# One activation-table set for Ln and Exp, chosen by the kernel: retention attention followed by a channel mix

## The chip, the core and the metric

The kernel runs on one core of one Trainium2 chip. The metric is device microseconds of one execution, as the median of the runs of a kernel; lower is better. Engines are called by the names that the profile uses: PE (TensorE), DVE (VectorE), ACT (ScalarE), POOL (GpSimd) and SP (the queue that issues the stores). PEld is the weight load of a matmul, which overlaps PE.

## The reference: what is computed

```python
def _attn_ref(q, k, v, g_norm):            # (8, 8, 576, 64) each, g_norm (64,)
    kv = np.einsum('bhsd,bhse->bhde', k, v)
    out = np.einsum('bhsd,bhde->bhse', q, kv)
    rms = np.sqrt(np.mean(out * out, axis=-1, keepdims=True) + 1e-06)
    return (out / rms * g_norm).astype(np.float32)

def _moe_ref(x, mu_k, mu_r, w_k, w_v, w_r):  # x (8, 576, 512), F = 1024
    x_prev = x shifted by one position, zero first
    xk = mu_k * x + (1.0 - mu_k) * x_prev
    xr = mu_r * x + (1.0 - mu_r) * x_prev
    k = np.maximum(xk @ w_k, 0.0)
    v = k * k @ w_v
    r = 1.0 / (1.0 + np.exp(-(xr @ w_r)))
    return (r * v).astype(np.float32)
```

The attention's output, heads side by side, is the x of the channel mix. Inputs and output are float32; the kernel works in bf16 with float32 sums.

## The kernel before, in words

The work comes in two kinds of pieces. `attention(b)` makes batch b ready: its k, v and q come by POOL's DMAs (L277); PE multiplies k by v into "kv" (L374) and transposes q (L402); PE multiplies q by kv (L421, "u"); copies take the results from PSUM to the tiles kvb, qT and uT (helper `copy`, L195 to L199, on ACT or on DVE); DVE squares u (L435); PE sums the squares over each head (L447, "ss"); ACT computes ln(ss/64 + 1e-6) (L450, `ln_act`) and exp(-0.5 ln), the reciprocal root (L453, `exp_act`), into the tile rs; DVE multiplies (L468, xT), takes differences (L479) and blends them with mu (L493, L496) into the rings xk and xr. All this is in pairs of heads: four pairs ("hp") in a batch, so four ln and four exp.

`mix(g)` takes 512 of the 4608 rows: k (L548, 32 matmuls), relu on ACT (L552), square on DVE (L555), r (L574, 16 matmuls), sigmoid on ACT (L578, `r_sig`), v (L601, 32 matmuls), the product with the sigmoid on DVE (L605, "out"), and the stores by SP (L531). There are nine groups g and eight batches b.

PSUM has two rings of two buffers each: "mm" for the mix, "at" for the attention. A kv, q or ss matmul has to wait until the "at" buffer of two pieces earlier has been read, which for ss is by ln; a k or v matmul waits in the same way for relu, sigmoid or out. The tile rs has one buffer.

The order of the instructions on each engine is written by `Planner` (L31 to L127). It takes every piece with its engine, an assumed duration and a due time, and picks the earliest. It knows two tables, "ln" and "sig" (pieces carry `table="ln"` or `table="sig"`), and adds `TABLE = 1.3` to a piece that changes between them; ln and exp have the same one. The order is then fixed, engine by engine. In the middle of the kernel one batch and one group are done in each round: sigmoid, then ln, ln, exp, exp twice (two pairs of heads each time), then relu and copies.

ACT computes functions from a table that has to be loaded (ACT_TABLE_LOAD). The kernel before asks for one load itself, at the start (L250, the set `natural_log_exp_and_others`, which holds both Ln and Exp); the other loads are put in by the compiler ahead of an ACTIVATE whose function is not in the set it last loaded. Those stand in the profile under the line of that ACTIVATE.

Of the kernel before, what the change touches and what calls it, by code (L numbers as in the profile page):

```python
# [30 lines left out]
class Planner:  # L31
# [10 lines left out]
    def add(self, on, fn, deps=(), bufs=(), due=0.0, rel=0.0, land=0.0, mode=None, table=None, name=""):  # L42
        p = Piece(on, fn, deps, bufs, due, rel, land, mode, table, name)
        self.left.append(p)
        return p
# [85 lines left out]
def kernel(  # L131
# [13 lines left out]
    nc = tc.nc  # L145
# [38 lines left out]
    add = plan.add  # L184

    def get(buf, dtype=None):
        if buf.t is None:
            n, shape, dt = BUFS[buf.tag]
            if dtype is not None:
                dt, shape = dtype, shape[:-1] + (shape[-1] * 2,)  # L190
            pool = psum if buf.tag in ("mm", "at") else sb
            buf.t = pool.tile(list(shape), dt, tag=buf.tag, name=buf.tag, bufs=n)
        return buf.t

    def copy(eng, dst, src):  # L195
        if eng == "ACT":
            nc.scalar.copy(out=dst, in_=src)  # L197
        else:
            nc.vector.tensor_copy(out=dst, in_=src)  # L199

    def act_us(n, sbuf=False, ap=False):
        return 0.1 + n / 1200 + (0.03 if sbuf else 0.0) + (0.09 if ap else 0.0)

# [28 lines left out]
    def first_load(n, eng):  # L232
        def fn(_):
            e = nc.sync if eng == "SP" else nc.scalar
            e.dma_start(out=first[n], in_=part(n, 0, 0, 2))
        return add({eng: 0.36}, fn, due=-2000, land=0.72, name="first" + n)

    def setup(_):
# [8 lines left out]
    f_k = first_load("k", "SP")  # L247
    f_v = first_load("v", "ACT")
    f_q = first_load("q", "SP")
    add({"ACT": 1.3}, lambda _: nc.scalar.preload_act_table_set("natural_log_exp_and_others"), due=-1999,  # L250
        table=None, name="table")
    p_set = add({"DVE": 1.4}, setup, due=-1999, name="setup")

    def small_loads(_):
# [8 lines left out]
    def cast(n, due):  # L263
        def fn(eng):
            copy(eng, get(kvq[(n, 0)])[:, 0:2, :], first[n])
        p = add({"DVE": dve_us(768, 2), "ACT": act_us(768, True)}, fn,
                deps=[{"k": f_k, "v": f_v, "q": f_q}[n], p_set], bufs=[kvq[(n, 0)]], due=due, name="cast" + n)
        for h in range(2):
            loaded[(n, 0, h)] = p
# [34 lines left out]
    def scale_w(dst, dep, due, name, on):  # L304
# [5 lines left out]
        return add(on, fn, deps=[dep, p_cols], due=due, name=name)  # L310

    both = {"DVE": dve_us(2048, 4), "ACT": act_us(2048, True, True)}
    p_wr = scale_w(w_r_sb, load_w(w_r_sb, moe_w_r, -700, 2.6, "w_r"), -50, "g.w_r", {"DVE": both["DVE"]})
    p_wk = []
# [25 lines left out]
    def attention(b):  # L340
# [9 lines left out]
        def when(stage, hp, pos=0):  # L350
            off, spread = STAGES[stage]
            if b == 0:
                return {"due": -200 + 6 * hp + off, "rel": 0.0}
            t = base + off + spread * hp
            return {"due": t, "rel": t - 4.0 if b > 2 else 0.0}
# [9 lines left out]
        for hp0, n in groups[1 if fine else 2 if b == 1 else 4]:  # L365
            ps = warm_ps if fine else Buf("at")
            hps = range(hp0, hp0 + n)
            o, bank = (HD * hp0, 1) if fine else (0, 0)

            def kv_mm(_, hps=hps, hp0=hp0, ps=ps, o=o, bank=bank):  # L370
                for hp in hps:
                    for j in range(NJ):
                        for e in range(2):
                            nc.tensor.matmul(  # L374
                                get(ps)[64 * e:64 * e + 64, bank, o + HD * (hp - hp0):o + HD * (hp - hp0) + HD],
                                kin.t[:, 2 * hp + e, HD * j:HD * j + HD], vin.t[:, 2 * hp + e, HD * j:HD * j + HD],
                                start=(j == 0), stop=(j == NJ - 1))

            def kv_cp(eng, e, hp0=hp0, n=n, ps=ps, o=o, bank=bank):
                rows_ = slice(64 * e, 64 * e + 64)  # L380
                copy(eng, kv[rows_, hp0:hp0 + n, 64 * e:64 * e + 64],
                     ps.t[rows_, bank, o:o + HD * n].rearrange("q (i d) -> q i d", d=HD))

            mm = add({"PE": 0.25 * n + 0.02}, kv_mm, bufs=[ps, kin, vin], mode="kv", name=f"kv{b}.{hp0}",
                     deps=[loaded[(m, b, h)] for m in ("k", "v") for h in (2 * hp0, 2 * (hp0 + n) - 1)],
                     **when("kv", hp0))
            cps = [add({"DVE": dve_us(64 * n), "ACT": act_us(64 * n)}, lambda eng, e=e, f=kv_cp: f(eng, e),
                       deps=[mm, p_set] + users, bufs=[ps], name=f"kvc{b}.{hp0}", **when("kvc", hp0))
                   for e in range(2)]
            for hp in hps:  # L390
                kvc[hp] = cps

        for hp0, n in groups[1 if fine else 2]:
# [11 lines left out]
            def q_cp(eng, hp0=hp0, n=n, ps=ps):  # L405
# [6 lines left out]
                    name=f"qc{b}.{hp0}", **when("qc", hp0))  # L412
# [3 lines left out]
        for hp in range(NHP):  # L416
# [7 lines left out]
            def u_cp(eng, hp=hp, ps=ps):  # L424
# [6 lines left out]
                         name=f"uc{b}.{hp}", **when("uc", hp))  # L431

        for hp0, n in groups[1 if b <= 1 else 2]:
            def u_sq(_, hs=slice(hp0, hp0 + n)):
# [3 lines left out]
                    name=f"sq{b}.{hp0}", **when("sq", hp0))  # L438
# [3 lines left out]
        for hp in range(NHP):  # L442
            ps, ln = Buf("at"), Buf("ln")

            def ss_mm(_, hp=hp, ps=ps):
                for i in range(2):
                    nc.tensor.matmul(get(ps)[:, i, 0:HS], ones, sq.t[:, hp, HS * i:HS * i + HS], start=True, stop=True)  # L447

            def ln_act(_, ps=ps, ln=ln):
                nc.scalar.activation(out=get(ln), in_=ps.t[:, :, 0:HS], func=AF.Ln, bias=eps, scale=1.0 / HD)  # L450

            def exp_act(_, hp=hp, ln=ln):
                nc.scalar.activation(out=get(rs)[:, hp].rearrange("q (i c) -> q i c", i=2), in_=ln.t, func=AF.Exp,  # L453
                                     scale=-0.5)

            m = add({"PE": 0.25}, ss_mm, deps=[sqc[hp], p_set], bufs=[ps, sq], mode="full", name=f"ss{b}.{hp}",
                    **when("ss", hp))
            a = add({"ACT": act_us(S, False, True)}, ln_act, deps=[m], bufs=[ps, ln], table="ln", name=f"ln{b}.{hp}",
                    **when("ln", hp))
            exps[hp] = add({"ACT": act_us(S, True)}, exp_act, deps=[a], bufs=[ln, rs], table="ln",  # L460
                           name=f"exp{b}.{hp}", **when("exp", hp))
# [72 lines left out]
    def mix(g):  # L534
# [23 lines left out]
        for f2 in range(NFC // 2):  # L558
            ps, rt, u = Buf("mm"), Buf("relu"), k0 + 2 * f2
            ms = []  # L560
            for x in range(2):
                ms.append(add({"PE": 0.865}, lambda _, fc=2 * f2 + x, ps=ps: k_mm(_, fc, ps),
                              deps=ms or need["k"] + [p_wk[f2 // 2]], bufs=[ps, sqk], due=u + x, mode="full",
                              name=f"k{g}.{2 * f2 + x}"))
            a = add({"ACT": act_us(1024)}, lambda _, ps=ps, rt=rt: k_relu(_, ps, rt), deps=ms[1:], bufs=[ps, rt],
                    due=u + 2, name=f"relu{g}.{f2}")
# [8 lines left out]
                                 start=(cc == 0), stop=(cc == NHP - 1))  # L575

        def r_sig(_, ps, sg):
            nc.scalar.activation(out=get(sg), in_=ps.t, func=AF.Sigmoid)  # L578

        sigs = []  # L580
        for c2 in range(2):
            ps, sg, u = Buf("mm"), Buf("sig"), r0 + 2 * c2
            ms = []
            if g == 0 and c2 == 0:
                for cc in range(NHP):
                    ms.append(add({"PE": 0.43}, lambda _, cc=cc, ps=ps: [r_mm(_, x, ps, [cc]) for x in range(2)],
                                  deps=ms[-1:] + [need["r"][cc], p_wr], bufs=[ps], due=u + 0.2 * cc, mode="full",
                                  name=f"r{g}.p{cc}"))
                ms = ms[-2:]
            else:  # L590
                for x in range(2):
                    ms.append(add({"PE": 0.865}, lambda _, ci=2 * c2 + x, ps=ps: r_mm(_, ci, ps, range(NHP)),
                                  deps=ms or need["r"] + [p_wr], bufs=[ps, sg], due=u + x, mode="full",
                                  name=f"r{g}.{2 * c2 + x}"))
            sigs.append((sg, add({"ACT": act_us(1024)}, lambda _, ps=ps, sg=sg: r_sig(_, ps, sg), deps=ms[1:],
                                 bufs=[ps, sg], due=u + 2, table="sig", name=f"sig{g}.{c2}")))
# [10 lines left out]
        for c2 in range(2):  # L607
# [3 lines left out]
            for x in range(2):  # L611
                for part_ in range(2):
# [3 lines left out]
                                  due=u + 2 * x + part_, mode="full", name=f"v{g}.{2 * c2 + x}.{part_}"))  # L616
# [45 lines left out]
```

## Time and profile before

| | |
|---|---|
| median of 3 runs | 249.96 us (249.74 to 249.97) |
| the profiled execution: its time | 250.53 us |
| its span | 248.8 us |
| busy: PE | 212.2 us (85%) |
| busy: ACT | 168.1 us (68%) |
| busy: DVE | 152.8 us (61%) |
| busy: POOL | 28.2 us (11%) |

The span is what the profiler sees from the first to the last instruction; the time has 1.73 us more around it. In a row of the timeline the first number is the start in us, the second the length of all instructions of the row together, then come the engine, the line, the operation, the tiles (out<-in), how many instructions were merged, and in brackets the idle time of the engine before it with what ended that idle time.

### The profile page before, as it was taken

The page shows a single profiled execution, that of the slowest core. Times are in us where ns is not written, and L with a number is a line of the kernel's source. Part 1 is how long each engine was busy: PE and PEld are TensorE (multiplying, and loading weights), DVE is VectorE, ACT ScalarE, POOL GpSimd, SP SyncE. Part 2 cuts the span into 40 slices and gives each one's busy share as a digit, 9 for nine tenths or more (in the row PEclk, how much of TensorE's full clock was granted, in tenths as well). Part 3 has the DMA queues.
Part 4 walks back from the last instruction along what each step waited for, and adds up shares of the span by engine and source line. Part 5 has one row for each costly group of instructions (what it writes and reads, how often), then busy time and mean ns, then how long its engine had stood idle before and what let it go on. Part 6 is the DMA issues. An engine that isn't in the chain of part 4 may idle for free.

```text
span 248.8 us, 4251 instructions
## 1 busy us (share of the span) xinstructions
PE 212.2 (85%) x1730; PEld 111.1 (45%) x1730; DVE 152.8 (61%) x287; ACT 168.1 (68%) x198; POOL 28.2 (11%) x43
## 2 busy tenths in 40 slices
PE   6784799598895859999699969996998999999981
PEld 6552345255442424455345656553453444444430
DVE  3279757479548668956991789369927943314221
ACT  2376349979799996899469957994899732513600
POOL 8932303023100001102010000000000000000000
PEclk9999999979998998999889999999999999999997
DMA  7999999999990229903990320033003205006023
GB/s 173 197 203 206 203 203 205 209 189 192 227 177 1 55 77 163 161 3 85 190 181 0 87 84 3 0 87 86 0 3 93 76 0 163 8 10 162 0 84 84
DMA packets 27431, 26.93 MB, mean 108 GB/s; under 512 B 1804, under 2 KB 22804, under 8 KB 27412
## 3 DMA queue, kind: packets, MB, share of 16 engines
q0 software_dynamic: 21008, 16.34, 43.6%
q1 hardware_dynamic: 6196, 10.04, 14.5%
q10 hardware_dynamic: 208, 0.29, 0.4%
q8 instruction: 13, 0.21, 0.3%
q14 instruction: 6, 0.05, 0.1%
HBM read 33.56 MB, written 9.44 MB: 173 GB/s over the span
## 4 chain that ended last, share of the span: by engine, by line
PE 45%; ACT 28%; DVE 15%; issue 5%; DMA 4%; SPq 1%; DVEq 0%; ACTq 0%
PE mm L548 18%; PE mm L601 11%; PE mm L574 8%; ACT L450 7%; ACT ln L450 7%; ACT rs L453 4%; ACT L453 3%; PE at L402 3%; ACT sig L578 2%; PE at L421 2%; DVE md L493 2%; DVE out L605 2%; DMA rows<-in_g_norm_dram 2%; DVE xr L496 2%; DVE qT L199 2%
## 5 line engine op out<-in xcount | busy, mean ns | idle before, releaser
L548 PE MATMUL mm<-xk,w_k 128*128 128x512 bf16 (+1 forms) x320 | 70.7, 367 | 3.6 <-DVE w_k L309 1.4
L601 PE MATMUL mm<-w_v,sqk 128*128 128x512 bf16 x288 | 68.9, 392 | 4.7 <-ACT sig L578 3.1
L552 ACT ACTIVATE relu<-mm 128x1024 bf16<-128x1024 f32 x36 | 36.7, 1022 | 38.3 <-PE mm L548 37.7
L605 DVE TENSOR_TENSOR out<-mm,sig 128x1024 f32<-128x1024 f32 (+1 forms) x20 | 22.3, 1116 | 40.8 <-PE mm L601 16.6
L601 PEld LDWEIGHTS <-sqk 128*128 128x128 bf16 x288 | 28.8, 100 | 38.3 <-issue 9.6
L548 PEld LDWEIGHTS <-w_k 128*128 128x128 bf16 x320 | 30.3, 99 | 32.8 <-issue 4.9
L574 PE MATMUL mm<-w_r,xr 128*128 128x512 bf16 x144 | 33.4, 379 | 3.7 <-DVE xr L496 2.8
L555 DVE TENSOR_TENSOR sqk<-relu 128x1024 bf16<-128x1024 bf16 x36 | 24.7, 687 | 14.7 <-ACT relu L552 14.5
L197 ACT CAST uT<-at 128x576 bf16<-128x576 f32 x24 | 15.0, 638 | 12.7 <-PE at L421 12.4
L468 DVE TENSOR_TENSOR xT<-uT,rs 128x1152 bf16<-128x1152 bf16 (+1 forms) x18 | 12.4, 690 | 17.9 <-ACT rs L453 17.9
L450 ACT ACTIVATE ln<-at,eps 128x576 f32<-128x576 f32 x32 | 22.4, 738 | 1.1 <-PE at L447 0.8
L578 ACT ACTIVATE sig<-mm 128x1024 bf16<-128x1024 f32 x18 | 18.2, 1024 | 7.0 <-PE mm L574 6.9
L574 PEld LDWEIGHTS <-xr 128*128 128x128 bf16 x144 | 13.8, 98 | 19.8 <-DVE xr L496 3.9
L493 DVE TENSOR_SCALAR md<-d,cols 128x576 bf16<-128x576 bf16 x64 | 21.2, 368 | 0.3
L453 ACT ACTIVATE rs<-ln 128x576 bf16<-128x576 f32 x32 | 20.5, 677 | 0.3
L453 ACT ACT_TABLE_LOAD x16 | 20.5, 1283 | 0.3
L450 ACT ACT_TABLE_LOAD x16 | 20.5, 1283 | 0.3
L421 PE MATMUL at<-qT,kvb 128*128 128x288 bf16 x64 | 13.8, 300 | 8.0 <-DVE qT L199 6.4
L277 POOL DMA_DIRECT2D k<-in_k_dram x11 | 8.1, 737 | 66.3 <-PE at L374 63.3
L435 DVE TENSOR_TENSOR sq<-uT 128x1152 bf16<-128x1152 bf16 (+1 forms) x20 | 12.6, 633 | 3.0 <-ACT uT L197 2.7
L199 DVE COPY qT<-at 128x1152 bf16<-128x1152 bf16 (+1 forms) x16 | 11.2, 700 | 3.7 <-PE at L402 3.6
L402 PE MATMUL at<-ident,q 96*64 96x96 bf16 x384 | 13.2, 223 | 0.0
(47 smaller groups left out, 161.5 us busy)
## 6 DMA issues: line engine op xcount, KB each, us to landing
out_dram<-out SPq DMA_DIRECT2D x24, 192.0 KB, 2.4
k<-in_k_dram POOLq DMA_DIRECT2D x6, 576.0 KB, 7.8
v<-in_v_dram POOLq DMA_DIRECT2D x6, 576.0 KB, 10.9
q<-in_q_dram POOLq DMA_DIRECT2D x6, 576.0 KB, 9.1
out_dram<-out SPq DMA_DIRECT2D x24, 128.0 KB, 2.4
out_dram<-out SPq DMA_DIRECT2D x24, 64.0 KB, 2.0
w_k<-in_moe_w_k_dram POOLq DMA_DIRECT2D x2, 512.0 KB, 10.5
w_v<-in_moe_w_v_dram POOLq DMA_DIRECT2D x1, 1024.0 KB, 15.9
```

Of the source, the lines that this page charges most:

```text
L402: nc.tensor.transpose(t[64 * e:64 * e + 64, hp - hp0, NP * j:NP * j + NP], qin.t[:, 2 * hp + e, HD * j:HD * j + HD], ident[:NP, :NP])
L421: nc.tensor.matmul(get(ps)[:, i, 0:HS], kv[:, hp, :], qT.t[:, hp, HS * i:HS * i + HS], start=True, stop=True)
L450: nc.scalar.activation(out=get(ln), in_=ps.t[:, :, 0:HS], func=AF.Ln, bias=eps, scale=1.0 / HD)
L453: nc.scalar.activation(out=get(rs)[:, hp].rearrange("q (i c) -> q i c", i=2), in_=ln.t, func=AF.Exp, scale=-0.5)
L493: nc.vector.tensor_scalar(out=get(md)[:, hp], in0=d.t[:, hp], scalar1=cols[:, m0 + hp:m0 + hp + 1], scalar2=None, op0=ALU.mult)
L548: nc.tensor.matmul(get(ps)[:, fc % 2, a0:a1], w_k_sb[:, cc, 128 * fc:128 * fc + 128], xk[:, cc, x0:x0 + a1 - a0], start=(cc == 0), stop=(c ...
L552: nc.scalar.activation(out=get(rt), in_=ps.t, func=AF.Relu)
L555: nc.vector.tensor_mul(out=get(sqk)[:, 2 * f2:2 * f2 + 2, :], in0=rt.t, in1=rt.t)
L574: nc.tensor.matmul(get(ps)[:, ci % 2, :], xr[:, cc, n0:n0 + 128], w_r_sb[:, cc, :], start=(cc == 0), stop=(cc == NHP - 1))
L578: nc.scalar.activation(out=get(sg), in_=ps.t, func=AF.Sigmoid)
L601: nc.tensor.matmul(get(ps)[:, ci % 2, :], sqk.t[:, fc, 128 * ci:128 * ci + 128], w_v_sb[:, fc, :], start=(fc == 0), stop=(fc == NFC - 1))
L605: nc.vector.tensor_mul(out=get(ot)[:, xs, :], in0=ps.t[:, xs, :], in1=sg.t[:, xs, :])
```

## The change

A helper `table(name)` remembers the set that the kernel asked for last, and asks for another one only where the name differs. It is called ahead of every Ln and Exp with `natural_log_exp_and_others`, ahead of every Sigmoid with `sigmoid_and_others`, and for the load at the start.

```diff
+    loaded_table = [None]
+
+    def table(name):
+        if loaded_table[0] != name:
+            loaded_table[0] = name
+            nc.scalar.preload_act_table_set(name)
...
-    add({"ACT": 1.3}, lambda _: nc.scalar.preload_act_table_set("natural_log_exp_and_others"), due=-1999,
-        table=None, name="table")
+    add({"ACT": 1.3}, lambda _: table("natural_log_exp_and_others"), due=-1999, name="table")
...
             def ln_act(_, ps=ps, ln=ln):
+                table("natural_log_exp_and_others")
                 nc.scalar.activation(out=get(ln), in_=ps.t[:, :, 0:HS], func=AF.Ln, bias=eps, scale=1.0 / HD)
 
             def exp_act(_, hp=hp, ln=ln):
+                table("natural_log_exp_and_others")
                 nc.scalar.activation(out=get(rs)[:, hp].rearrange("q (i c) -> q i c", i=2), in_=ln.t, func=AF.Exp,
                                      scale=-0.5)
...
         def r_sig(_, ps, sg):
+            table("sigmoid_and_others")
             nc.scalar.activation(out=get(sg), in_=ps.t, func=AF.Sigmoid)
```

On ACT, in a round in the middle of the kernel, this stands in the queue before (sig is the sigmoid of a group, ln and rs the logarithm and the exponential of a batch, x2 two pairs of heads):

```order
L578 ACT_TABLE_LOAD
L578 ACTIVATE sig<-mm 128x1024 x2
L450 ACT_TABLE_LOAD
L450 ACTIVATE ln<-at,eps 128x576 x2
L453 ACT_TABLE_LOAD
L453 ACTIVATE rs<-ln 128x576 x2
L450 ACT_TABLE_LOAD
L450 ACTIVATE ln<-at,eps 128x576 x2
L453 ACT_TABLE_LOAD
L453 ACTIVATE rs<-ln 128x576 x2
L197 CAST kvb_74<-at 64x4x64
```

And this is the same place with the change (its lines are numbered a little higher, and all loads have the line of the helper):

```order
L206 ACT_TABLE_LOAD
L587 ACTIVATE sig<-mm 128x1024 x2
L206 ACT_TABLE_LOAD
L457 ACTIVATE ln<-at,eps 128x576 x2
L461 ACTIVATE rs<-ln 128x576 x2
L457 ACTIVATE ln<-at,eps 128x576 x2
L461 ACTIVATE rs<-ln 128x576 x2
L197 CAST kvb_74<-at 64x4x64
```

Three of the five loads of the round are gone, and nothing has changed places. Over the whole queue of ACT, 14 loads stand where 40 stood: 1 at the start, 7 ahead of sigmoids, 6 ahead of a Ln. PE, DVE, POOL and SP have the same instructions in the same order as before.

## Prediction

> **What bounds the kernel now.** I read the page first: the busy times, the engine shares of the chain that ended last, and the groups of table loads.
>
> ```profile
> PE 212.2 (85%) x1730; PEld 111.1 (45%) x1730; DVE 152.8 (61%) x287; ACT 168.1 (68%) x198; POOL 28.2 (11%) x43
> ...
> PE 45%; ACT 28%; DVE 15%; issue 5%; DMA 4%; SPq 1%; DVEq 0%; ACTq 0%
> ...
> L453 ACT ACT_TABLE_LOAD x16 | 20.5, 1283 | 0.3
> L450 ACT ACT_TABLE_LOAD x16 | 20.5, 1283 | 0.3
> ```
>
> The groups by line of ACT give the other loads.
>
> ```profile
> L578 ACT ACT_TABLE_LOAD x7 | 9.0, 1283 | 0.1
> ...
> L250 ACT ACT_TABLE_LOAD x1 | 1.3, 1283 | 1.2 <-PEq L646 1.2
> ```
>
> 40 loads of 1.283 us are 51.3 of ACT's 168.1 us. ACT is not the busiest engine, but it is 28% of the chain. So the question is where PE, the busiest, stands still because of ACT. PE's waits:
>
> ```profile
> PE at L421 <- DVE qT L199: 6.4, 3, 2.2
> PE at L374 <- ACT ln L450: 5.7, 2, 2.9
> PE mm L601 <- ACT sig L578: 3.1, 1, 3.1
> ```
>
> The first is ACT at second hand, as the rounds below show: that DVE copy is late because DVE waited for rs.
>
> **The change.** It removes 26 loads (14 stay), 26 x 1.283 = 33.4 us of ACT. It moves nothing, adds no wait, and no DMA is touched. What is gained is not 33.4 but what PE no longer waits; so I went along the timeline and asked at each wait of PE what is late next. First, Ln and Exp from the joint set cost nothing extra. In batch 0, both run from it already; the chain of waits has
>
> ```profile
> 13.68 0.75 ACT ln L450
> 14.46 0.69 ACT rs L453
> ```
>
> against 0.74 and 0.68 for the later ones (45.50 below, and half of 1.37 for a pair), and exp starts 0.03 us after the ln that it reads. So a removed load is worth its whole slot on ACT.
>
> *Group 0 and batch 1, to 55 us.* The timeline:
>
> ```profile
> 44.21 1.28 ACT L450 ACT_TABLE_LOAD   x1
> 45.50 0.74 ACT L450 ACTIVATE ln<-at,eps 128x576 f32<-128x576 f32 x1
> 46.26 1.28 ACT L453 ACT_TABLE_LOAD   x1
> 48.26 1.28 ACT L450 ACT_TABLE_LOAD   x1
> 49.55 1.37 ACT L450 ACTIVATE ln<-at,eps 128x576 f32<-128x576 f32 x2
> 50.34 0.95 PE L374 MATMUL at<-v,k 96*64 96x64 bf16 x48 [2.78 <-ACT ln L450]
> 52.03 3.23 PE L601 MATMUL mm<-w_v,sqk 128*128 128x512 bf16 x8
> ...
> 83.20 1.89 PE L601 MATMUL mm<-w_v,sqk 128*128 128x512 bf16 x8
> ```
>
> The kv matmul at 50.34 waits for the first ln of the pair. The ln at 45.50 comes 1.28 earlier with the load at 44.21 gone, and I add 0.3 because the copy in front of it also moves up; then two more loads go: 1.28 + 0.3 + 2 x 1.28 = 4.1. What is late next is PE itself (eight v matmuls and an ss that also sat behind ln), which I put 0.4 later: **+3.7**. Behind this wait the eight matmuls at 52.03 took 3.23 us, where the same eight at 83.20 took 1.89: they ran at half speed after PE stood still. With the wait gone I count 3.23 - 1.89 = **+1.3**. Then DVE becomes late: its xT, d, xr and out rows run on without a gap, and the squares that feed the next ss come, by my count, 1.2 after PE wants them: **-1.2**. Sum 3.8.
>
> *Group 1, to 83 us.*
>
> ```profile
> 60.24 1.28 ACT L450 ACT_TABLE_LOAD   x1
> ...
> 62.29 1.28 ACT L453 ACT_TABLE_LOAD   x1
> ...
> 65.23 1.02 PE L548 MATMUL mm<-xk,w_k 128*128 128x512 bf16 x4 [1.02 <-ACT relu L552]
> ...
> 71.15 1.28 ACT L450 ACT_TABLE_LOAD   x1
> ...
> 73.21 1.28 ACT L453 ACT_TABLE_LOAD   x1
> ...
> 77.57 5.30 PE L601 MATMUL mm<-w_v,sqk 128*128 128x512 bf16 x16 [3.06 <-ACT sig L578]
> ```
>
> The two loads ahead of 65.23 (2.6 us) hide PE's wait of 1.02 for relu entirely: **+1.0**. The v matmuls at 77.57 wait for the sigmoid; two loads go in front of it, 2.57, of which I take 2.3 (a Ln waits for its ss instead): **+2.3**, and PE keeps a wait of 0.7. The sixteen at 77.57 took 5.30 at half speed against 3.6 (twice 1.89, less their overlap): **+1.7**. Sum 8.8.
>
> *Batch 3, to 107 us.*
>
> ```profile
> 81.13 1.28 ACT L453 ACT_TABLE_LOAD   x1
> ...
> 85.78 0.41 PE L447 MATMUL at<-sq,ones 128*128 128x288 bf16 x2 [0.69 <-ACT ln L450]
> ...
> 88.95 1.28 ACT L450 ACT_TABLE_LOAD   x1
> ...
> 91.03 0.95 PE L374 MATMUL at<-v,k 96*64 96x64 bf16 x48 [2.88 <-ACT ln L450]
> ...
> 91.92 3.26 PE L548 MATMUL mm<-xk,w_k 128*128 128x512 bf16 x8
> ```
>
> Four loads go from 81.13 to 88.95, 5.1 us of ACT, more than the two waits of PE (0.69 + 2.88); about 0.3 stays, because the ss ahead has to come first: **+3.3**. The eight at 91.92 are at half speed again, 3.26 - 1.89 = **+1.4**. From there to 107 DVE works without a gap, and the second copy of qT comes 0.7 after PE wants it: **-0.7**. Sum 12.8.
>
> *The rounds of batches 4 to 6, then batch 7.* Of the round of batch 5 the timeline has:
>
> ```profile
> 135.95 1.28 ACT L453 ACT_TABLE_LOAD   x1
> 138.51 1.28 ACT L450 ACT_TABLE_LOAD   x1
> 138.53 0.76 DVE L468 TENSOR_TENSOR xT<-uT,rs 128x1152 bf16<-128x1152 bf16 x1 [1.06 <-ACT rs L453]
> 143.78 0.76 DVE L468 TENSOR_TENSOR xT<-uT,rs 128x1152 bf16<-128x1152 bf16 x1 [0.85 <-ACT rs L453]
> 148.23 0.41 PE L421 MATMUL at<-qT,kvb 128*128 128x288 bf16 x2 [2.07 <-DVE qT L199]
> ```
>
> Three loads go from the round, so the second rs comes 3.85 earlier, but DVE has its own work: it only loses its two waits, 1.06 + 0.85 = 1.91. Everything from the second xT to the qT copy is DVE without a gap, so u comes 1.9 earlier and PE's 2.07 becomes about 0.2. I take **+1.9** for the round of batch 4 and **+1.85** each for the next two. In the round of batch 4 the wait of u was 2.21 and slow matmuls followed, in the others not:
>
> ```profile
> 122.66 0.41 PE L421 MATMUL at<-qT,kvb 128*128 128x288 bf16 x2 [2.21 <-DVE qT L199]
> ...
> 124.10 1.89 PE L548 MATMUL mm<-xk,w_k 128*128 128x512 bf16 x4
> ```
>
> Four of those are 1.03 at 65.23 above; with the transposes beside them **+1.1**. Sum 12.8 + 1.9 + 1.1 + 3.7 = 19.5. In batch 7 the wait that matters is
>
> ```profile
> 191.47 4.69 PE L548 MATMUL mm<-xk,w_k 128*128 128x512 bf16 x21 [1.20 <-DVE out L605]
> ```
>
> an "out" that sits behind the xT that waits for rs: **+1.1**. From 191.47 on PE has only mix matmuls and nothing changes. Total **20.6 us**: span 248.8 - 20.6 = 228.2, time 250.53 - 20.6 = **229.9 us** by the profiled execution's own time, which is 0.57 above the median of the runs shown; against that median I would say 229.4 and keep 229.9.
>
> The Trainium skill ("ScalarE: Activation LUTs", What ACT_TABLE_LOAD costs) gives a switch 1283 ns for the load and about 1380 ns more for a drain, 2.66 us in all; by that the 26 loads would free an estimated 69 us of ACT and not 33.4. The trace agrees with the 1283 and shows no drain: the load at 46.26 starts 0.02 after its ln ends, and the pair of ln at 49.55 starts 0.01 after the load.
>
> Half-speed matmuls are 1.3 + 1.7 + 1.4 + 1.1 = 5.5 of the 20.6. They follow waits of PE of 2.78, 3.06, 2.88 and 2.21, and not the one of 2.07; the longest wait that I leave is 0.7. The skill's "TensorE: Matmul & The Clock Gate" (What's actually happening) has the clock halved after an idle window of about 3.4 us, free-running; by it, too, waits of 0.7 would keep full speed and the sum stays. The trace is harsher than the page: 2.21 was enough.
>
> **The rivals.**
> *The clock still drops* (chance 0.09). PE's waits come back elsewhere, over 2 us, and slow matmuls follow as now: 229.9 + 5.5 = 235.4. For: four of five such waits had them. Against: the waits that I find left are below 0.8.
>
> *VectorE takes the early gain* (0.09). DVE has few gaps from 50 to 60 and 90 to 107, and I followed it by hand. If half of the 12.8 up to 107 is eaten by DVE's order, 229.9 + 6.4 = 236.3. Against: its total, 152.8, is far below PE's 212.2.
>
> *Slower: a denser PE is given a lower clock* (0.02). After the change PE runs with hardly a gap. If its 212.2 us went at 0.83, the clock of the first row below, that would cost 212.2 x (1/0.83 - 1) = 43 us: 229.9 + 43 = 273. It decides below a clock of 0.91 (212.2 x 0.097 = 20.6). Against it is the second row, a stretch in which PE never paused:
>
> ```profile
> 120.00:130.00 10.00, 7.79 (x54) 3.97 (x52) 9.44 (x18) 4.94 (x7) 0.77 (x1) 0.83 1.22 207
> ...
> 200.00:210.00 10.00, 10.00 (x48) 4.41 (x46) 2.85 (x3) 2.14 (x3) 0.00 (x0) 1.00 0.22 60
> ```
>
> The number behind POOL's count is PEclk, the granted clock: 0.83 where PE had stood still and slow matmuls followed, 1.00 where it was busy throughout.
>
> *The loads come back* (0.01): the compiler or the hardware loads again ahead of each Exp, and the time stays at 250. The program's order has 14 loads, so I give it little.
>
> **How the numbers follow.** The forecast has 0.79. Range: at the low end the two give-backs of DVE (1.9) and the waits left (0.7, 0.3, three of 0.2, and a little) don't come, 229.9 - 4.4 = 225.5; at the high end it takes in the clock rival and almost the DVE one: 236. A measurement of this kernel tells about 0.2% from no change. Faster 0.97 (forecast and the first two rivals), same 0.01, slower 0.02.
>
> **What would show it.** Right: 14 loads in the profile after, ACT near 168.1 - 33.4 = 134.7 busy, no wait of PE over 1 us for ln or sigmoid between 40 and 190, rounds of batches 5 and 6 about 1.9 us shorter each, no eight 512-column matmuls over 2.5 us there, and the tail from the last ln to the end as long as now. Wrong: a new wait of PE for DVE of more than 1 us in each round (then the DVE terms are too small), slow matmuls still in the middle (then the clock term is), or a Ln or Exp longer than 0.75.

## The result and the profile after

The changed kernel takes **228.15 us** (median of 4 runs, 227.13 to 228.74) against 249.97 us for the kernel before (4 runs, 249.74 to 250.84): ratio 0.9117, interval 0.9077 to 0.9157, 21.8 us less. The forecast was 229.9, with a range of 225.5 to 236. The profiled execution is the fastest of the four, 227.13 us with a span of 225.3; before it was 250.53 and 248.8. So this pair of traces differs by 23.5 in span, 1.7 more than the medians do, and every number from the traces below has to be read with that in mind. Some executions of the kernel before fell into a slower state, and the ratios and the times of before in the experiments go by the others.

The page of the profile after: busy times, the engines' shares of the chain, and the loads, which now all have the helper's line.

```profile
PE 206.6 (92%) x1730; PEld 108.7 (48%) x1730; DVE 152.3 (68%) x287; ACT 133.8 (59%) x172; POOL 28.1 (12%) x43
...
PE 58%; DVE 27%; ACT 5%; DMA 4%; SPq 2%; issue 1%; DVEq 0%
...
L206 ACT ACT_TABLE_LOAD x14 | 18.0, 1283 | 1.4 <-PEq L655 1.2
```

ACT is 5% of the chain, where it was 28%, and 34.3 us less busy (134.7 was forecast; 133.8 it is). PE has 58% of the chain (45% before) and DVE 27% (15% before). The waits of PE:

```profile
PE mm L582 <- DVE xr L504: 3.0, 3, 1.4
PE mm L610 <- DVE out L614: 1.7, 2, 0.8
...
PE mm L610 <- ACT sig L587: 0.8, 1, 0.8
...
PE at L427 <- DVE qT L199: 0.4, 2, 0.2
```

The three that led the list before are 0.8 (sigmoid), 0.4 (qT) and gone (kv). What is left for a Ln or a sigmoid is one wait of 0.8 us; waits for ACT's copies are 1.5 us together, as before. Where the time came from can be read from starts of the same instruction in both traces. From the timeline of before, the ones that the prediction did not show:

```profile
28.97 5.35 PE L548 MATMUL mm<-xk,w_k 128*128 128x512 bf16 x24 [1.43 <-DVE w_k L309]
...
106.85 3.62 PE L601 MATMUL mm<-w_v,sqk 128*128 128x512 bf16 x16
...
132.51 3.62 PE L601 MATMUL mm<-w_v,sqk 128*128 128x512 bf16 x16
...
152.81 3.62 PE L574 MATMUL mm<-w_r,xr 128*128 128x512 bf16 x16
...
177.05 3.62 PE L574 MATMUL mm<-w_r,xr 128*128 128x512 bf16 x16
...
244.05 0.69 DVE L605 TENSOR_TENSOR out<-mm,sig 128x512 f32<-128x512 f32 x1 [1.11 <-PE mm L601]
```

And from the timeline after (its lines for k, v, r and out are L556, L610, L582 and L614):

```profile
28.64 5.35 PE L556 MATMUL mm<-xk,w_k 128*128 128x512 bf16 x24
...
46.16 0.95 PE L380 MATMUL at<-v,k 96*64 96x64 bf16 x48
...
47.56 1.90 PE L610 MATMUL mm<-w_v,sqk 128*128 128x512 bf16 x8
...
69.36 3.61 PE L610 MATMUL mm<-w_v,sqk 128*128 128x512 bf16 x16 [0.80 <-ACT sig L587]
...
77.33 0.95 PE L380 MATMUL at<-v,k 96*64 96x64 bf16 x48
...
78.21 1.90 PE L556 MATMUL mm<-xk,w_k 128*128 128x512 bf16 x8
...
92.09 3.62 PE L610 MATMUL mm<-w_v,sqk 128*128 128x512 bf16 x16
...
114.43 3.62 PE L610 MATMUL mm<-w_v,sqk 128*128 128x512 bf16 x16
...
132.63 3.62 PE L582 MATMUL mm<-w_r,xr 128*128 128x512 bf16 x16
...
154.76 3.62 PE L582 MATMUL mm<-w_r,xr 128*128 128x512 bf16 x16
...
220.59 0.69 DVE L614 TENSOR_TENSOR out<-mm,sig 128x512 f32<-128x512 f32 x1 [1.11 <-PE mm L610]
```

Measured from the first k matmul of group 0 (which came 0.33 earlier by itself), the marks are earlier by:

| mark | before, us | after, us | earlier by | the prediction's sum there |
|---|---|---|---|---|
| kv of batch 2 | 50.34 | 46.16 | 3.9 | 3.7 |
| v of group 1 | 77.57 | 69.36 | 7.9 | 7.1 |
| kv of batch 4 | 91.03 | 77.33 | 13.4 | 12.1 |
| v of group 2 | 106.85 | 92.09 | 14.4 | 12.8 |
| v of group 3 | 132.51 | 114.43 | 17.8 | 15.8 |
| r of group 4 | 152.81 | 132.63 | 19.9 | 17.7 |
| r of group 5 | 177.05 | 154.76 | 22.0 | 19.5 |
| last out | 244.05 | 220.59 | 23.1 | 20.6 |

The eight matmuls behind the kv took 1.90 (3.23 before), the sixteen of group 1 3.61 (5.30), the eight behind the kv of batch 4 1.90 (3.26).

### The profile page after: what moved, and what is told of

It reads as the page before. It is cut to its first block, busy times and chain, and to the rows that moved or that the text cites. A ratio compares the mean times of both kernels' runs of the same rounds, so it can differ in the third digit from the quotient of the medians.

```text
span 225.3 us, 4225 instructions
## 1 busy us (share of the span) xinstructions
PE 206.6 (92%) x1730; PEld 108.7 (48%) x1730; DVE 152.3 (68%) x287; ACT 133.8 (59%) x172; POOL 28.1 (12%) x43
## 4 chain that ended last, share of the span: by engine, by line
PE 58%; DVE 27%; ACT 5%; DMA 4%; SPq 2%; issue 1%; DVEq 0%
PE mm L556 19%; PE mm L610 19%; PE mm L582 13%; DVE out L614 6%; DVE md L501 4%; DVE qT L199 3%; DVE xT L476 3%; DVE d L487 3%; PE at L427 3%; DMA out_dram<-out 3%; DVE xk L504 2%; PE at L408 2%; DVE xr L504 2%; DMA rows<-in_g_norm_dram 2%; DVE sqk L563 2%; PE at L453 2%
## 5 line engine op out<-in xcount | busy, mean ns | idle before, releaser
L556 PE MATMUL mm<-xk,w_k 128*128 128x512 bf16 (+1 forms) x320 | 68.6, 358 | 0.5 <-DVE xk L504 0.5
L610 PE MATMUL mm<-w_v,sqk 128*128 128x512 bf16 x288 | 65.9, 379 | 2.5 <-DVE out L614 1.7
L614 DVE TENSOR_TENSOR out<-mm,sig 128x1024 f32<-128x1024 f32 (+1 forms) x20 | 22.3, 1116 | 38.1 <-PE mm L610 13.9
L610 PEld LDWEIGHTS <-sqk 128*128 128x128 bf16 x288 | 28.1, 98 | 33.8 <-issue 3.5
L556 PEld LDWEIGHTS <-w_k 128*128 128x128 bf16 x320 | 29.9, 98 | 28.3 <-issue 1.4
L582 PE MATMUL mm<-w_r,xr 128*128 128x512 bf16 x144 | 34.9, 392 | 3.9 <-DVE xr L504 3.0
L582 PEld LDWEIGHTS <-xr 128*128 128x128 bf16 x144 | 14.2, 101 | 21.1 <-DVE xr L504 4.1
L461 ACT ACTIVATE rs<-ln 128x576 bf16<-128x576 f32 x32 | 20.6, 687 | 0.2
L206 ACT ACT_TABLE_LOAD x14 | 18.0, 1283 | 1.4 <-PEq L655 1.2
L504 DVE TENSOR_TENSOR xk<-md,xT 128x1152 bf16<-128x1152 bf16 (+1 forms) x18 | 12.5, 692 | 0.6
L504 DVE TENSOR_TENSOR xr<-md,xT 128x1152 bf16<-128x1152 bf16 (+1 forms) x18 | 12.5, 692 | 0.6
```

The costliest lines, as they stand in the source:

```text
L504: nc.vector.tensor_tensor(out=dst[:, hs, c0:c0 + S], in0=md.t[:, hs], in1=xT.t[:, hs, 0:S], op=ALU.add)
L556: nc.tensor.matmul(get(ps)[:, fc % 2, a0:a1], w_k_sb[:, cc, 128 * fc:128 * fc + 128], xk[:, cc, x0:x0 + a1 - a0], start=(cc == 0), stop=(c ...
L582: nc.tensor.matmul(get(ps)[:, ci % 2, :], xr[:, cc, n0:n0 + 128], w_r_sb[:, cc, :], start=(cc == 0), stop=(cc == NHP - 1))
L610: nc.tensor.matmul(get(ps)[:, ci % 2, :], sqk.t[:, fc, 128 * ci:128 * ci + 128], w_v_sb[:, fc, :], start=(fc == 0), stop=(fc == NFC - 1))
L614: nc.vector.tensor_mul(out=get(ot)[:, xs, :], in0=ps.t[:, xs, :], in1=sg.t[:, xs, :])
```

## The experiments

Theory A is the prediction's: a load costs its slot on ACT and nothing else, PE's waits and the slow matmuls behind them carry it to the end, and after the change PE paces. Each kernel was timed beside the kernel before on the same chip, but there were three chips in all, so between experiments the ratios compare better than the times. "Rival C" below is the reading that the gain is a price per load.

**Half of the loads each.** The first keeps the joint set up to batch 3, the second from batch 4 on (and in batch 0). Both for Ln; the same condition with `exp_and_others` stands ahead of Exp:

```diff
-                table("natural_log_exp_and_others")
+                table("natural_log_exp_and_others" if b < 4 else "natural_log")
```

```diff
-                table("natural_log_exp_and_others")
+                table("natural_log_exp_and_others" if b == 0 or b >= 4 else "natural_log")
```

> The joint set for batches 0 to 3 alone; from batch 4 on Ln and Exp load a set each, as before: 26 loads, 14 fewer than before. Theory A, the gain lies where PE waited (in the trace after, v of group 2 starts 14.4 us earlier than before, measured from the first k matmul): 235 to 236.5 us. Rival C, every load is worth the same (21.8 us over 26 loads, 0.84 each): 238.2 us.

> The joint set for batch 0 and from batch 4 on; batches 1 to 3 load for each Ln and each Exp, as before: 28 loads, 12 fewer than before. Theory A: the four later rounds give what is left of 21.8 after 14.4, 7.4 to 8.7 us: 241.3 to 242.6 us, and the slow matmuls at 52, 77 and 92 us stay while those at 124 go. Rival C, by the number of loads (12 x 0.84): 239.9 us.

Measured: 236.29 us (ratio 0.9434, 0.9392 to 0.9476) and 242.09 (0.9678, 0.9633 to 0.9723), before 250.22. Both lie where theory A had them. The early loads are worth 13.9 us, 14 of them, 1.0 each; the later ones 8.1, 12 of them, 0.7 each; together 22.1, the whole change. Rival C, 238.2 and 239.9, lies outside both intervals. The waits of PE in the two, early only and late only:

```profile
PE at L427 <- DVE qT L199: 6.6, 4, 2.2
```

```profile
PE at L380 <- ACT ln L457: 4.0, 2, 2.8
PE at L453 <- ACT ln L457: 3.2, 2, 2.4
...
PE mm L610 <- ACT sig L587: 3.1, 1, 3.1
```

Each half has the waits of its own loads and not those of the other. One thing of the second kernel's expectation missed: the matmuls that run slowly in the kernel before at 52, 77 and 92 us do so here only in the first place. The sixteen of group 1 stand behind the same wait as before, 3.06 us, and keep full speed; two times four matmuls behind the next wait are slow in their stead (four take 1.03 at full speed):

```profile
80.10 3.61 PE L610 MATMUL mm<-w_v,sqk 128*128 128x512 bf16 x16 [3.06 <-ACT sig L587]
...
88.31 0.41 PE L453 MATMUL at<-sq,ones 128*128 128x288 bf16 x2 [2.38 <-ACT ln L457]
88.55 1.66 PE L610 MATMUL mm<-w_v,sqk 128*128 128x512 bf16 x4
...
90.48 1.88 PE L610 MATMUL mm<-w_v,sqk 128*128 128x512 bf16 x4
```

**A copy in place of each load.** At the 26 places ACT copies a bf16 tile that nobody reads; `fn` and `was` find the places where the kernel before loads.

```diff
...
+    def slot_copy():
+        nc.scalar.copy(out=slot_dst, in_=slot_src.rearrange("p (o n) -> p o n", o=1).broadcast_to([128, 2, 700]))
...
         if loaded_table[0] != name:
             loaded_table[0] = name
             nc.scalar.preload_act_table_set(name)
+        elif changed:
+            slot_copy()
```

> The changed kernel with an ACT copy of 128x1400 bf16 at each of the 26 places from which a table load went. By the copies of 128x576 and 128x1152 in the trace of before (639 and 1119 ns, 0.833 ns an element) such a copy should last about 1.33 us and overlap its neighbours a little, so that it holds ACT about as long as a load (1.28). Theory A, a load costs its slot on ACT and nothing else: 249 to 252 us, the time of before, with PE's waits of 2.8 to 3.1 us at the kv and v matmuls back. Rival B, a load costs much more than its slot (a drain, a refill): only part of the gain is given back, 238 to 243 us.

Measured: 246.3 us (ratio 0.9836, 0.9785 to 0.9886): between the two theories, nearer to A, and within neither's range. The timeline of this kernel says why: a copy overlaps what stands before and behind it.

```profile
44.99 0.75 ACT L470 ACTIVATE ln<-at,eps 128x576 f32<-128x576 f32 x1
45.63 1.36 ACT L209 COPY slot_dst<-slot_src 128x1400 bf16<-128x1400 bf16 x1
46.88 0.69 ACT L474 ACTIVATE rs<-ln 128x576 bf16<-128x576 f32 x1
```

From the start of ln to the start of its exp are 1.89 us, against 2.05 with a load (45.50 to 47.55 in the kernel before) and 0.77 or 0.78 without anything (40.60 to 41.37 after; 13.68 to 14.46 before). So the copy adds 1.12 and the load 1.28. This was a fault of my sizing, not yet an answer; with 1592 elements (796 in place of 700) the copy should add 1.28.

> As the first experiment, with copies of 128x1592. There a copy of 1400 added 1.12 us from the start of a Ln to the start of its Exp (1.89 against 0.77), a load 1.28 (2.05 against 0.77), because a copy overlaps its neighbours and a load does not. 192 elements more are 0.16 us, so that now each place adds 1.28. Theory A, a load costs its slot on ACT and nothing else: the time of before, 249 to 251 us. Rival B, a load costs something beside its slot: the time stays below 248.

Measured: 250.79 us against 249.54 for before, ratio 1.0067 (1.0015 to 1.0118), inside theory A's 249 to 251. From the start of a Ln to the start of its Exp are now 2.04 us (41.12 to 43.16), as with a load. The waits of PE in this kernel, which has the changed kernel's 14 loads:

```profile
PE at L440 <- DVE qT L199: 6.3, 3, 2.2
PE at L393 <- ACT ln L470: 4.0, 2, 2.8
PE at L466 <- ACT ln L470: 3.2, 2, 2.4
PE mm L624 <- ACT sig L601: 3.1, 1, 3.1
```

They come at the places of before and add up to the same: 6.3 for qT (6.4 before), 3.1 for the sigmoid, and 7.2 for the Ln of kv and ss together. Only the share of ss has grown, from 1.5 to 3.2, at the cost of kv, as in the kernel with the late set alone. The whole gain is given back by holding ACT as long as a load does, with none of the 26 loads there: a load's cost is its slot. Rival B falls. (Why it ends 0.7% above before, and not level with it, stays open.)

**No change of set at all.** Exp stands in place of Sigmoid in the gate, so that one load is left and the gate's values are not the sigmoid's.

```diff
-            table("sigmoid_and_others")
-            nc.scalar.activation(out=get(sg), in_=ps.t, func=AF.Sigmoid)
+            table("natural_log_exp_and_others")
+            nc.scalar.activation(out=get(sg), in_=ps.t, func=AF.Exp)
```

> The changed kernel with Exp in place of Sigmoid in the gate, so that one load at the start is the only one (13 fewer); the gate's values are then exp and not the sigmoid. Theory A, after the change PE paces and ACT is off the path: only the v matmuls of group 1, which wait 0.80 us for the sigmoid, and about as much elsewhere: 226.5 to 227.8 us. Rival D, ACT's loads still pace the kernel, 0.84 us each as before: about 217 us.

Measured: 226.95 us (ratio 0.9078, 0.9035 to 0.9122), 1.2 below the first runs of the change and 0.6 below its second ones (further down). 13 loads less are worth at most about 0.1 us each now, where the 26 were worth 0.8. ACT is all but off the path, and rival D falls.

**The clock of PE.** One, two or three copies of 128x1400 stand ahead of the first sigmoid of group 1, the only one for which PE still waits:

```diff
...
         def r_sig(_, ps, sg):
+            if g == 1 and ps is sig_ps[0]:
+                for _i in range(2):
+                    slot_copy()
             table("sigmoid_and_others")
```

> The changed kernel with one ACT copy of 128x1400 (about 1.3 us) ahead of the first sigmoid of group 1, for which PE waits 0.80 us there. Theory A, with the clock of PE falling after a wait of over 2 us: the wait becomes about 2.1, close to the bound that before showed (2.07 without, 2.21 with slow matmuls); if the clock holds, the sixteen v matmuls last 3.6 us and the kernel takes 1 to 1.4 us more: 229.2 to 229.6 us. Rival E, PE's clock has nothing to do with its waits: the same.

> The same with two copies: the wait becomes about 3.4 us. Theory A: the sixteen v matmuls run at half speed for most of their length, 5.3 us in place of 3.6, and the kernel takes 2.6 + 1.7 = 4.3 us more than the changed one, less what later slack takes: 231.5 to 232.5 us. Rival E: 3.6 us for the sixteen and 2 to 2.6 us more: 230.2 to 230.8 us.

> Three copies of 128x1400 ahead of the first sigmoid of group 1: PE's wait for it grows from 3.4 to about 4.7 us. Theory A: the sixteen v matmuls last 5.3 us as with two copies, since the clock has fallen already, and only the wait grows: 1.2 to 1.4 us more than with two, 232.4 to 232.7 us. Rival G, slow matmuls grow with the wait: 5.3 us or more for the sixteen and slow ones after them, over 233 us.

Measured: 228.74, 231.24 and 233.83 us (ratios 0.9132, 0.9233, 0.9373, each about 0.4% either way). The first is a little below what was expected, and the second lies between the expectations of theory A and of rival E, so that the times alone don't decide. The v matmuls of group 1 in the three timelines:

```profile
71.83 3.61 PE L622 MATMUL mm<-w_v,sqk 128*128 128x512 bf16 x16 [2.05 <-ACT sig L597]
```

```profile
72.43 5.30 PE L622 MATMUL mm<-w_v,sqk 128*128 128x512 bf16 x16 [3.44 <-ACT sig L597]
```

```profile
73.66 6.27 PE L622 MATMUL mm<-w_v,sqk 128*128 128x512 bf16 x16 [4.83 <-ACT sig L597]
```

After 2.05 us of waiting the sixteen are as fast as after 0.80; after 3.44 they take 1.69 us more, as in the kernel before; after 4.83 another 0.97. Rival E falls. But my own expectation for the third, that the loss stays at 1.7 once the clock has fallen, missed as well: by this trace and by the time, 2.6 us more than with two copies for 1.4 us of waiting (3.5 us by the ratios), rival G is nearer. It is one trace of each, and the last section shows how far one place can differ between traces. The granted clock of the third falls to 0.59 (stretches from 70 to 75 and 75 to 80 us):

```profile
70.00:75.00 5.00, 1.34 (x4) 0.52 (x4) 3.04 (x7) 4.97 (x5) 0.00 (x0) 0.72 0.37 57
75.00:80.00 5.00, 5.00 (x16) 1.90 (x15) 0.00 (x0) 3.32 (x5) 0.00 (x0) 0.59 0.00 0
```

In the first step of the time, 0.6 to 1.2 us for 1.3 of waiting, the run-to-run spread of about 1% is too wide to say more.

> The changed kernel as it is, beside the others on the same chip: 227.5 to 228.7 us. The one copy was 0.6 us and the two copies 3.1 us above the 228.15 of its first runs; here the base of these two differences is measured again.

Measured: 227.56 us against 249.54, ratio 0.9145 (0.911 to 0.9181): the result stands.

**The kernel before, kept warm.** 40, 44 and 40 matmuls of zeros fill three of PE's waits; they write PSUM columns that are overwritten, or that nobody reads.

```diff
...
+    def keep_warm(buf, c0, n):
+        for _i in range(n):
+            nc.tensor.matmul(get(buf)[:, 1, c0:c0 + 128], zero[:, 0:128], zero[:, 128:256], start=True, stop=True)
...
             def kv_mm(_, hps=hps, hp0=hp0, ps=ps, o=o, bank=bank):
+                if b in (2, 4):
+                    keep_warm(warm_at["kv%d" % b], 0, 40)
...
         def v_mm(_, ci, part, ps):
...
+            if g == 1 and ci == 0 and part == 0:
+                keep_warm(warm_at["ss2"], 320, 44)
```

> The kernel before, all 40 loads in it, with 40, 44 and 40 matmuls of zeros (128 columns) on PE in the three waits ahead of the kv of batch 2, the v of group 1 and the kv of batch 4, so that PE doesn't stand still there for more than about 0.7 us. Their results are overwritten and change nothing. Theory A, the clock falls because PE stood still: the matmuls behind run at full speed (8 in 1.9 and 16 in 3.6 us), but most of the 4.4 us that they save lie beside ACT, which is busy with its loads then, so that the time falls by 1 to 2.5 us: 247.5 to 249 us. Rival F, the slow matmuls count in full, as the sum of the prediction has them: 245.6 us. Rival E, the clock has nothing to do with the waits: 250 us and slow matmuls as before.

Measured: 249.02 us against 249.78, ratio 0.9972 (0.9941 to 1.0003): 0.8 us less by the medians, with an interval that just includes nothing, and less than the 1 to 2.5 us that theory A had here. The trace decides more than the time:

```profile
50.92 1.90 PE L615 MATMUL mm<-w_v,sqk 128*128 128x512 bf16 x8
...
75.85 3.61 PE L615 MATMUL mm<-w_v,sqk 128*128 128x512 bf16 x16 [0.60 <-ACT sig L588]
...
84.05 0.64 PE L454 MATMUL at<-sq,ones 128*128 128x288 bf16 x2 [2.38 <-ACT ln L457]
84.48 1.91 PE L615 MATMUL mm<-w_v,sqk 128*128 128x512 bf16 x4
...
86.67 1.42 PE L615 MATMUL mm<-w_v,sqk 128*128 128x512 bf16 x4
...
90.25 0.95 PE L381 MATMUL at<-v,k 96*64 96x64 bf16 x48
91.13 1.90 PE L556 MATMUL mm<-xk,w_k 128*128 128x512 bf16 x8
```

All three groups run at full speed where PE no longer stands still. But of the 1.7 us that the sixteen save, nothing arrives: the next ss waits 2.38 us for ln in place of 0.69, and two times four matmuls behind that run slowly instead. The kv of batch 4 starts at 90.25 where it started at 91.03, and this trace's first k matmul was 0.81 earlier by itself: nothing of the first two groups is left. ACT, full of loads, was late there anyway. So rival F, the slow matmuls counted in full, falls for the kernel before.

## Why the prediction was right

**The loads.** 14 are left, each 1283 ns, and a load takes its slot on ACT and no more: right, and shown by the two copy experiments. The prediction's remark against the drain of the Trainium skill ("ScalarE: Activation LUTs", What ACT_TABLE_LOAD costs: about 1380 ns beside the load) stands: 1.28 us of a plain copy in each place restores the old time, where 2.66 would have needed twice that.

**The terms to 107 us.** Each was right in place and in order, and each stretch of the table came out small, by 0.2 to 0.6 us: 14.4 against 12.8. The largest misses are the kv of batch 4, of which I left a wait of 0.3 and which has none after, and the two give-backs to DVE, -1.2 and -0.7. DVE did come late there, but less: where I had 1.2, PE waits after the change 0.3 for the squares and 0.5 for xk, and where I had 0.7, 0.2 for qT.

**The rounds.** I took 1.85 us for each of two rounds and the traces give 2.1 for both (19.9 - 17.8 and 22.0 - 19.9), because PE's waits of 2.07 and 2.12 for qT went entirely. The term's mechanism was right: in before DVE's xT waited 17.3 us for rs in all, now 1.1. Before and after, the group of xT:

```profile
L468 DVE TENSOR_TENSOR xT<-uT,rs 128x1152 bf16<-128x1152 bf16 x14 | 10.6, 758 | 17.3 <-ACT rs L453 17.3
```

```profile
L476 DVE TENSOR_TENSOR xT<-uT,rs 128x1152 bf16<-128x1152 bf16 x14 | 10.5, 750 | 1.1 <-ACT rs L461 1.1
```

**The slow matmuls, 5.5 us.** They are gone in the trace after. That PE's standing still brings them is supported by the delays and the warm kernel, and from 30 us to the last few us the changed kernel's clock is 1.00 in both of its traces. Three things in the prediction's words were wrong. First, they were written as terms that stand by themselves; the warm kernel shows that in the kernel before the 1.7 of group 1 is worth nothing, since ACT is late behind it, and so it counts only together with the loads that go. Second, I read a bound out of one trace, "2.21 was enough" and 2.07 not. There is none: the same wait of 3.05 or 3.06 us was followed by 5.30 in the kernel before and by 3.61 with the late set alone and with the longer copies. Third, the trace of before has six such waits of over 2 us and not five: I left out one of 2.12 at 172.48, behind which the matmuls kept full speed. The 5.5 us are what one execution had. In the executions of the kernel before whose mean granted clock is listed it lies between 0.940 and 0.967, and the profiled one has 0.967; so most others lost more clock over the whole span, and not less. Where, and what it cost them, is not on record.

**The total.** 20.6 us against 21.8 by the medians, and 23.5 between the two profiled executions, the second of which was the shortest of its four. By the traces, from which the sum was made, it was 2.5 short; that it comes within 1.2 of the medians is in part luck of the executions. PE left with hardly a wait also answers the rivals: the clock does not drop, a dense PE is not given less, and DVE takes back 0.8 and 0.2 us up to 107 and not half of the gain, although its part of the chain has grown to 27%. My 0.2% for what a measurement can tell was too fine: executions of the kernel before went from 247.4 to 251.7 us.

**The signs.** All that the prediction named as right came, but for one: from the end of the last ln to the end of the span are 60.8 us and not the 59.1 of before. The last ln came earlier by more than the end did, since PE and not ACT paces there.

## What to carry to other kernels

Look for table loads between functions that one set could hold: here, once the first sigmoid had replaced the joint set that the kernel had asked for at its start, the compiler loaded at every change between Ln and Exp, and naming that set ahead of each use took 26 of 40 loads away. Then price a load by who waits for the slot behind it and not by its length: here one was worth 1.0 us in the first half, 0.7 in the rounds, and 0.1 after PE had become the bound. A wait of PE of about 2 us and more can cost more than itself; but add the slow matmuls behind it to a sum only where nothing else is late at their end, and not as a fixed price.

## What the runs showed of the hardware

Whether PE's matmuls run slowly after a wait is not decided by its length alone. From 30 us on they kept full speed after every wait of up to 1.6 us, and after 2.05 to 2.12 us in all places but one; at 2.2 and at 3.05 us both happened; after 2.37 to 2.88 us they were slow each time; and in the kernel with the shorter copies a wait of 1.71 was enough, shortly behind it:

```profile
120.07 0.40 PE L440 MATMUL at<-qT,kvb 128*128 128x288 bf16 x2 [1.71 <-DVE qT L199]
...
121.04 1.89 PE L569 MATMUL mm<-xk,w_k 128*128 128x512 bf16 x4
```

With the early loads alone gone, on the other hand, a wait of 2.21 had no consequence:

```profile
108.28 0.41 PE L427 MATMUL at<-qT,kvb 128*128 128x288 bf16 x2 [2.21 <-DVE qT L199]
...
109.25 1.04 PE L556 MATMUL mm<-xk,w_k 128*128 128x512 bf16 x4
```

The Trainium skill ("TensorE: Matmul & The Clock Gate", What's actually happening) has a window of about 3.4 us that runs free of the kernel. That the same wait goes both ways fits a window whose place relative to the kernel changes; that 1.71 us can be enough does not fit a rule of a whole idle window, and neither do the other slow places behind waits shorter than 3.4. It is an argument, since no run here moved the window by itself.

The start of the kernel is a case of its own. Behind a wait of 1.38 us at 25 us, ten r matmuls took 2.33 us in the kernel before and in its warm copy, and 3.65 to 4.45 in all ten traces of kernels with the helper. Why is not known. The changed kernel's first k matmul came no later for it, at 28.64 us: in the kernel before, PE waited 1.43 us for w_k there and started it at 28.97.

Matmuls of zeros kept the clock up as real ones do, in all three places where they stood. And a table load does not overlap its neighbours on ACT, while a copy does, by about 0.1 us at each end. That is why copies of 1.36 us added only 1.12, 0.16 less than a load, and 192 elements had to be added before the copies stood for the loads.
